# Loading 112 of 128 rows of four token blocks ahead, and 16 later, at the seam of a fused long convolution and soft mixture of experts

## The chip, the cores and the metric

The program runs on one core of a Trainium2 chip. The metric is the device time of one execution in microseconds, the median of three: 898.48 us (896.55 to 900.4) before the change.

## What is computed

A long convolution with a gate makes the tokens; a soft mixture of experts, whose softmaxes run over all tokens (dispatch) and over all slots (combine), works on them.

```python
# x, v: (4, 11456, 128); h_filt: (11456, 128) from pos_emb, w1, w2 and a decay
u = x * v
y = irfft(rfft(u, 2*S) * rfft(h_filt, 2*S))[:S]
x = (x * y).reshape(45824, 128)
logits = x @ phi                                  # (45824, 32): 8 experts with 4 slots
d = softmax(logits, axis=0)                       # over the tokens
slot_input = (d.T @ x).reshape(8, 4, 128)
slot_out = relu(slot_input @ w1[e]) @ w2[e]       # F = 1024
out = softmax(logits, axis=1) @ slot_out
```

## The kernel before

**Convolution.** The 128 features are worked in 8 groups of 16 (`CG`), by transforms in four steps that run as matrix products. Step g of the outer loop (`for g in range(G + 1)`, L476) does the first two steps of group g and the last two of group g - 1. The large region `T` holds a group's spectra; the third step `p3` (L353) reads it and writes `E`; the fourth, `p4` (L397), reads `E`, once for each of seven row blocks `rb` in the order `ORDER`; `p4_gate` or `p4_gate_apart` multiply its result with the input `x`; `p4_out` (L449) writes the products to `scr` in DRAM, a buffer in pieces, each of which holds all 128 features of a range of tokens. Group g fills rows 16 g to 16 g + 15 of each piece. In the last turn, g = 8, no first step is left: all third steps of the last group run (L537), and then the seven fourth steps.

**Mixture.** The 45,824 tokens are 23 blocks of 16 tiles of 128 tokens (the last has 6). A block is loaded from `scr` as 128 rows (features) of 2048 tokens, 8192 B a row. `Moe.load` (L685) does it for a block and a range of rows, with one DMA for each piece that the block touches, on SP's queue. Blocks 0 to 4 have buffers in the region of the table `W`, which is free earlier (`ahead_buf`, L659). Blocks 5 to 8 have theirs in the region of `T` (`xreg`, made by `places`, L675), which is free when the last third step has read `T`; block 9 has one in `E`. Blocks from 10 on use the buffers of blocks 5 to 9 again. The expert weights `w1` go into the region of blocks 0 to 4 when those have been used.

For blocks 0 to 4 rows 0 to 111 (groups 0 to 6, `D - CG` = 112) are loaded by `weights` (L661) before the last third steps, and rows 112 to 127 by `ahead` (L716) when the last group's products are in `scr`. `ahead(t)` runs behind the products of row block number t: blocks 0 and 1 at t = 1, blocks 2 to 5 at t = 2, 6 and 7 at t = 3, 8 at t = 4, 9 at t = 5. Blocks 5 to 9 are loaded there whole.

The generator `_moe` (L726) holds the dispatch: for pairs of blocks, `logits` (L768) multiplies the block with `phi`, a running maximum, exponentials, `turn` (L697), which transposes the block on TensorE, and `dispatch` (L858), which adds up the slots. The logits of the pair 0, 1 are computed between the sixth and the seventh fourth step, the others behind the seventh; VectorE's gates of the sixth and seventh fourth step come behind the first logits. `fetch` (L949) follows each `turn`: behind blocks 0 to 3 it loads `w1` (L664), behind block 4 `w2` (L667), and from block 5 on block i + 5.

**Order.** Computing instructions keep the order in which they are written (`keep_in_program_order`). The DMAs go through SP's queue in an order that the framework's planner makes from its own costs, and which follows the program for the most part. Dependences are kept by semaphores that the framework sets. The edge rows `ex` (L571) are 128 x 12 floats, 6 KB.

Of the kernel before, what the change touches and what calls it, by code (L numbers as in the profile page):

```python
# [17 lines left out]
B, S, D = 4, 11456, 128  # L18
# [11 lines left out]
CG = D // G  # L30
# [33 lines left out]
def conv_part(ctx, tc, cp, moe, xf, vf, xi, xe, pos, w1, w2, win, t1x, t1h, wt, t3, t4, hs, scr):  # L64
# [190 lines left out]
    def p1_x(g, u):  # L255
        if g == 0 and u < NU // 2:
            xt = moe.E[:, J * N1 + 8 * RP * u :][:, : 8 * RP].rearrange("p (c q r) -> p c q r", c=2, q=4)
        elif g == 0 and u >= NU - 6:
            xt = m_half(g, u).rearrange("p (c q r) -> p c q r", c=2, q=4)
        else:  # L260
            xt = ld.tile([128, 2, 4, RP], F32, tag="ld", name=f"x_{g}_{u}")
        inorder(nc.sync.dma_start(out=xt, in_=xf[g, u]))
        xts[u] = xt
# [66 lines left out]
    def p1(g, u, sd, large=False):  # L330
        first_out(g, u, first(g, u, sd, large))
# [52 lines left out]
    def p4_load(g, rb):  # L384
        t = spare[next(turns) % len(spare)]
        inorder(nc.sync.dma_start(out=t, in_=xi[g, rb]))
        return t
# [88 lines left out]
    for g in range(G + 1):  # L476

        if g == 0:
            for u in range(NU):
                p1(g, u, sds.pop(u))  # L480
                if u in (9, 11):
                    p1_x(1, PRE + 2 + (u - 9) // 2)
        elif g < G:
            if not pso:
                first_ps.close()
                pso.append(conv_ps.enter_context(tc.tile_pool(name="pso", bufs=2, space=bass.MemoryType.PSUM)))
            def third(us, larges):
                for u, large in zip(us, larges):
                    p3(g - 1, u, large)
                    if u + 2 < NU and u + 2 not in sds:  # L490
                        sds[u + 2] = p1_sd(g, u + 2, nc.vector)

            def behind(u):
                w = u + 6
                if w < NU:
                    p1_x(g, w)
                elif w < NU + PRE and g + 1 < G:
                    p1_x(g + 1, w - NU)

            def spectrum(i0, i1):  # L500
                for k in range(11 * i0, 11 * i1, 11):
                    inorder(nc.sync.dma_start(out=Hs[:HP, k : k + 11], in_=hs[g - 1, :, k : k + 11]))

            large = g > 1
            ps = [first(g, u, sds[u], not large) for u in range(2)]
            third(range(2), (large, large))
            for u in range(2):
                first_out(g, u, ps[u])
                behind(u)
            for w in range(PRE + HV, NU):  # L510
                p1_v(g, w)
            third(range(2, 4), (large, large))
            for u in range(2, 4):
                p1(g, u, sds[u], not large)
                behind(u)
            for b in range(1, NU // 4):
                if b > 1:
                    spectrum(4 * b - 8, 5 * b - 6)
                us = range(4 * b, 4 * b + 4)
                third(us, (large, large, not large, not large))  # L520
                for u in us:
                    p1(g, u, sds[u], large == (u % 4 < 2))
                    behind(u)
            if g + 1 < G:
                for w in range(PRE):
                    p1_v(g + 1, w)
        else:
            x0, x1, x2 = [sm.tile([128, PW], F32, tag="m", name=f"xl_{i}", bufs=3) for i in range(3)]
            spare = [x0, x1, x2] + [spare[i % 2] for i in (next(turns), next(turns))] + [x0, x2]
            turns = count()  # L530
            xvs = [p4_load(g - 1, rb) for rb in ORDER[:5]]
            moe.weights()
            conv_ps.close()
            moe.logit_banks()
            pso[0] = ctx.enter_context(tc.tile_pool(name="psl", bufs=3, space=bass.MemoryType.PSUM,
                                                    reuse_waits="tile"))
            for u in range(NU):  # L537
                p3(g - 1, u)
            moe.places()
            moe.steps = _moe(moe)  # L540
            next(moe.steps)

        sds = {}
        nxt_g = g + 1 if g + 1 < G else None

        def ahead(step):
            if nxt_g is None:
                return
            if step == 1:
                for u in range(PRE):  # L550
                    sds[u] = p1_sd(nxt_g, u, nc.vector)
            else:
                for u in range(PRE, PRE + 4):
                    p1_x(nxt_g, u)

        if 0 < g:
            ahead(1)
        ks = list(range(0, J, KB)) if g < G else []
        if g == 0:
            sds = next_sds  # L560
            for i, k in enumerate(ks):
                if k % HK == 0:
                    for w in range(k, min(J, k + HK), 4):
                        filter_last(w)
                p2(g, k)
                if i in (1, 5, 9, 13):
                    u = PRE + i // 4
                    sds[u] = p1_sd(1, u, nc.vector)
            continue
        ex = exs[g % 2]  # L570
        inorder(nc.sync.dma_start(out=ex, in_=xe[g - 1]))  # L571
        if g < G:
            xvs = {0: p4_load(g - 1, 0), APART: p4_halves(g - 1, APART), 2: p4_load(g - 1, 2)}
            vcs, done = {}, 0
            for what, n in STEPS:
                if what == "p2":
                    for _ in range(n):
                        p2(g, ks[done])
                        done += 1
                elif what != "gate":  # L580
                    pv = p4(g - 1, n, what)
                    if what:
                        vcs[n] = p4_copy(g - 1, n, pv)
                else:
                    if n == APART:
                        p4_gate_apart(n, xvs[n], pvs[n], vcs[n], ex)
                    else:
                        p4_gate(g - 1, n, xvs[n], pvs[n], vcs[n], ex)
                    if g < G - 1 and n == 5:
                        for u in range(PRE, PRE + HV):  # L590
                            p1_v(g + 1, u)
                    p4_out(g - 1, n, xvs[n])
                    if n == 0:
                        ahead(2)
                    if n in NEXT:
                        xvs[NEXT[n]] = p4_load(g - 1, NEXT[n])
                    if n == 2:
                        xvs[6] = p4_halves(g - 1, 6)
            assert done == len(ks)
            p4_rest(g - 1, ex)  # L600
            continue
        def last_gate(t, rb, xv, pv, vc):
            if t < 4:
                p4_gate(g - 1, rb, xv, pv, vc, ex)
            else:
                p4_gate_apart(rb, [xv[:, PW // 2 * w :][:, : PW // 2] for w in range(2)], pv, vc, ex)
            p4_out(g - 1, rb, xv)
            if t == 5:
                p4_rest(g - 1, ex)
            if t == 3:  # L610
                xvs.append(p4_load(g - 1, ORDER[6]))
            moe.ahead(t)
            if t == 1:
                xvs.append(p4_load(g - 1, ORDER[5]))

        for t, rb in enumerate(ORDER):
            p4(g - 1, rb, 0)
            if t == 6:
                next(moe.steps)
                last_gate(*held)  # L620
            pv = p4(g - 1, rb, 1)
            vc = p4_copy(g - 1, rb, pv)
            held = (t, rb, xvs.pop(0), pv, vc)
            if t == 4:
                moe.spot = wide[rb][:, 0, 2 * NJ : 2 * NJ + 8]
            if t >= 5:
                next(moe.steps)
            if t != 5:
                last_gate(*held)


class Moe:
# [83 lines left out]
    def ahead(self, t):  # L716

        if t == 0:
            make_identity(self.tc.nc, self.ident)
            self.tc.keep_in_program_order(self.tc.nc.vector.tensor_reduce(  # L720
                out=self.mask, in_=self.ident.rearrange("p (a s) -> p a s", a=4), axis=AX.X, op=ALU.add))
        for i in ((), (0, 1), (2, 3, 4, 5), (6, 7), (8,), (9,), ())[t]:
            self.load(i, D - CG if i < self.XB else 0)


def _moe(mo):  # L726
# [564 lines left out]
```

## Time and profile before

| what | us |
|---|---|
| median of three runs | 898.48 |
| the three runs | 896.55, 898.48, 900.4 |
| the profiled execution, time | 899.17 |
| the profiled execution, span from first to last instruction | 897.4 |
| TensorE (PE) busy in it | 858.3 (96%) |
| VectorE busy | 716.3 (80%) |
| ScalarE busy | 454.7 (51%) |
| GpSimd busy | 392.7 (44%) |

The profile is of one execution. Busy times say how much of the span an engine had an instruction at work; a busy share near 100% doesn't say that nothing waits, since it is a mean over stages. [...] The DMA share is the mean busy share of the 16 DMA engines, and can come out a little over 1 because transfers of one engine overlap. SP is the engine that issues the DMAs; its queue's rows are marked SPq.

### The profile page before, as it was taken

What the parts mean: (1) busy time and instruction counts of PE and PEld (TensorE: products, weight loads), DVE (VectorE), ACT (ScalarE), POOL (GpSimd) and SP (SyncE); (2) the same over time, 40 slices, a digit from 0 to 9 for tenths busy, and PEclk for the clock granted to TensorE, in tenths of its full rate; (3) what the DMA queues carried; (4) which work ended last, traced back from release to release, by engine and by line L of the source; (5) the groups of instructions that cost most, each with busy time, mean ns of one, the idle gap of its engine ahead of it and who ended that gap; (6) DMA issues with size and microseconds to landing.
All of it is one profiled execution on the core that took longest, in us unless ns stands there. A gap on an engine that the chain in (4) does not pass through costs nothing. (4 is left out here: it accounts for less than half of the span.)

```text
span 897.4 us, 37454 instructions
## 1 busy us (share of the span) xinstructions
PE 858.3 (96%) x16264; PEld 792.2 (88%) x16264; DVE 716.3 (80%) x1239; ACT 454.7 (51%) x971; POOL 392.7 (44%) x538
## 2 busy tenths in 40 slices
PE   9999999999999999999999999999999999599991
PEld 9998989999999999999999999999999987376640
DVE  5967966898899899979988998898697078396791
ACT  5775557316712841581175148216612548497761
POOL 4004850591096039207802940691096015395750
PEclk9999999999999999999999999999999999699996
DMA  9954675548647655874675567557527979893698
GB/s 328 396 185 132 209 231 168 159 132 261 200 128 225 214 159 167 257 210 125 191 249 163 148 212 248 162 147 247 169 60 214 256 224 382 335 317 122 265 417 367
DMA packets 96114, 197.02 MB, mean 220 GB/s; under 512 B 14649, under 2 KB 56539, under 8 KB 92750
## 3 DMA queue, kind: packets, MB, share of 16 engines
q1 hardware_dynamic: 95774, 194.50, 67.2%
q8 instruction: 128, 2.10, 1.0%
q14 instruction: 36, 0.29, 0.1%
q10 hardware_dynamic: 144, 0.07, 0.0%
q0 software_dynamic: 32, 0.07, 0.0%
HBM read 137.73 MB, written 56.86 MB: 217 GB/s over the span
## 5 line engine op out<-in xcount | busy, mean ns | idle before, releaser
L350 POOL TENSOR_TENSOR T<-m 111x256 f32<-111x256 f32 (+1 forms) x199 | 150.3, 755 | 344.1 <-DVE m L344 343.8
L344 DVE TENSOR_TENSOR m<-p,T 111x1024 f32<-111x1024 f32 (+1 forms) x175 | 200.4, 1205 | 14.8 <-POOL T L351 7.8
L360 PE MATMUL p<-tab,T 111*99 111x112 f32 x2048 | 205.4, 261 | 1.4 <-POOL T L351 0.3
L360 PEld LDWEIGHTS p<-tab,T 111*99 111x99 f32 x2048 | 198.8, 170 | 6.4 <-issue 1.6
L340 PE MATMUL p<-T,W 128*64 128x128 f32 (+1 forms) x3168 | 198.1, 276 | 0.3 <-issue 0.3
L420 ACT ACTIVATE vc<-p 128x416 f32<-128x416 f32 x112 | 51.8, 515 | 266.5 <-PE p L411 220.4
L340 PEld LDWEIGHTS p<-T,W 128*64 128x64 f32 (+1 forms) x3168 | 183.2, 127 | 2.2 <-issue 0.5
L411 PE MATMUL p<-tab,E 99*64 99x104 f32 x3584 | 176.0, 252 | 1.2 <-DVE E L373 0.6
L411 PEld LDWEIGHTS p<-tab,E 99*64 99x64 f32 x3584 | 168.2, 136 | 3.4 <-ACT vc L420 0.8
L375 ACT ACTIVATE E<-p 99x448 f32<-99x448 f32 x254 | 131.8, 575 | 64.3 <-PE p L360 58.2
L351 POOL TENSOR_TENSOR T<-m 111x256 f32<-111x256 f32 (+1 forms) x199 | 146.7, 737 | 0.0
L186 ACT ACTIVATE T<-p 128x396 f32<-128x396 f32 x240 | 100.2, 537 | 11.2 <-PE p L174 11.1
L174 PE MATMUL p<-tab1x,x 53*64 53x99 f32 x3648 | 86.8, 246 | 0.2 <-ACT E L224 0.2
L174 PEld LDWEIGHTS p<-tab1x,x 53*64 53x64 f32 x3648 | 79.8, 132 | 4.4 <-ACT E L224 0.4
L436 DVE TENSOR_TENSOR p<-p,vc 128x832 f32<-128x832 f32 x46 | 47.2, 1027 | 10.1 <-ACT vc L420 10.1
L268 DVE TENSOR_TENSOR x<-x,T 128x448 f32<-128x448 f32 x51 | 31.5, 618 | 20.3 <-DMA x<-in_xf_dram 12.6
L714 ACT ACTIVATE xreg<-pt 128x512 f32<-128x512 f32 (+1 forms) x68 | 35.0, 608 | 12.3 <-PE pt L708 12.2
L270 DVE TENSOR_TENSOR T<-x 128x224 f32<-128x224 f32 x102 | 39.2, 426 | 1.7
L274 DVE TENSOR_TENSOR x<-T 128x224 f32<-128x224 f32 x102 | 39.2, 425 | 1.8
L224 ACT ACTIVATE E<-fl 111x512 f32<-111x512 f32 (+1 forms) x50 | 26.8, 627 | 21.4 <-PE fl L218 21.4
L444 DVE TENSOR_TENSOR E<-p,E 128x824 f32<-128x824 f32 x36 | 36.6, 1017 | 1.2
L344 DVE TENSOR_TENSOR m<-p,E 111x1024 f32<-111x1024 f32 (+1 forms) x25 | 28.7, 1202 | 5.1 <-PE p L340 4.9
(156 smaller groups left out, 972.3 us busy)
## 6 DMA issues: line engine op xcount, KB each, us to landing
x<-in_xf_dram SPq DMA_DIRECT2D x114, 256.0 KB, 4.0
out_dram<-xreg SPq DMA_DIRECT2D x16, 1024.0 KB, 10.7
E<-in_xi_dram SPq DMA_DIRECT2D x37, 412.0 KB, 4.0
T<-in_vf_dram SPq DMA_DIRECT2D x65, 224.0 KB, 4.8
scr<-E SPq DMA_DIRECT2D x67, 206.0 KB, 3.8
T<-hs SPq DMA_DIRECT2D x63, 154.0 KB, 4.7
hs<-E SPq DMA_DIRECT2D x12, 784.0 KB, 4.6
mv<-in_vf_dram SPq DMA_DIRECT2D x42, 224.0 KB, 4.6
```

What stands on the lines that cost most here:

```text
L174: inorder(nc.tensor.matmul(ps[h][RP * d : RP * d + RP, i, s, :], lhsT=sd[js, i, s, d, :], rhs=tab1x[js, J * (s + d) : J * (s + d + 1)], st ...
L186: inorder(nc.scalar.activation(dst, src, AF.Copy))
L270: inorder(eng.tensor_tensor(out=vt[:, :, m : m + 2], in0=xr[:, :, 0:2], in1=xr[:, :, 2:4], op=op))
L340: inorder(nc.tensor.matmul(ps[ns, i].rearrange("p b c -> p (b c)"), lhsT=W[:, k0 + i, ns], rhs=Tf[:, :, k0 + i, :], start=True, stop=True, ...
L344: inorder(nc.vector.tensor_mul(m[:, :n].rearrange("p k s e c i -> p k s (e c i)").rearrange("p k s (b c) -> p k s b c", c=CG), ps[:, :n].u ...
L350: inorder(eng.tensor_tensor(out=Ty[:, 0], in0=m[:, :n, 0, 0], in1=m[:, :n, 1, 1], op=ALU.subtract))
L351: inorder(eng.tensor_tensor(out=Ty[:, 1], in0=m[:, :n, 1, 0], in1=m[:, :n, 0, 1], op=ALU.add))
L360: inorder(nc.tensor.matmul(pk[:, i, 2 * s : 2 * s + 2, :].rearrange("p q r -> p (q r)"), lhsT=T[0:N1, s, 2 * k + i, u // 2, :, u % 2], rhs ...
L375: inorder(nc.scalar.activation(dst, src, AF.Copy))
L411: inorder(nc.tensor.matmul(pv[RP * h : RP * h + RP, 2 * k + i, w, :], lhsT=E[:J, r, 2 - 2 * w + s, :], rhs=tab4[:, s, o : o + NJ], start=( ...
L420: inorder(nc.scalar.activation(vc[:, w], pv[:, :, 0, :], AF.Copy, scale=2.0 * w - 1.0))
L436: inorder(nc.vector.tensor_tensor(out=pw, in0=pw[:, 1:2].to_broadcast([128, 2, 4, NJ]), in1=vc, op=ALU.add))
```

## The change

The loads of rows 0 to 111 (seven groups) of blocks 5 to 8 are written right behind the last third step, where the region of `T` has become `xreg`. In `ahead`, where these blocks were loaded whole, only rows 112 to 127 are loaded, as for blocks 0 to 4. Block 9 is loaded whole as before. With the pieces that they touch, blocks 5 to 8 took 6 DMAs and now take 12.

```diff
@@ -537,6 +537,8 @@
             for u in range(NU):
                 p3(g - 1, u)
             moe.places()
+            for i in range(moe.XB, 2 * moe.XB - 1):
+                moe.load(i, 0, D - CG)
             moe.steps = _moe(moe)
             next(moe.steps)
 
@@ -720,7 +722,7 @@
             self.tc.keep_in_program_order(self.tc.nc.vector.tensor_reduce(
                 out=self.mask, in_=self.ident.rearrange("p (a s) -> p a s", a=4), axis=AX.X, op=ALU.add))
         for i in ((), (0, 1), (2, 3, 4, 5), (6, 7), (8,), (9,), ())[t]:
-            self.load(i, D - CG if i < self.XB else 0)
+            self.load(i, D - CG if i < 2 * self.XB - 1 else 0)
 
 
 def _moe(mo):
```

`XB` is 5, so the ranges are blocks 5 to 8, and i < 9.

## Rows read from the trace of the kernel before

**Rows 1.** The page, the span in 40 slices of 22.4 us, in tenths.

```profile
PE   9999999999999999999999999999999999599991
PEclk9999999999999999999999999999999999699996
DMA  9954675548647655874675567557527979893698
```

**Rows 2.** Chain of waits in time, 740 to 790: start us, us, what.

```profile
743.42 1.92 PE pl L774 x16
...
749.88 1.92 PE pl L774 x16
...
752.44 8.04 DMA ffw<-in_mw_dram
...
760.54 11.72 DMA xreg<-scr
...
772.40 1.97 PE pl L774 x8
...
782.38 1.92 PE pl L774 x16
```

**Rows 3.** Windows: length, busy by engine, then granted clock, DMA share, GB/s.

```profile
704.00:718.00 14.00, 13.44 (x188) 13.26 (x188) 0.94 (x3) 7.76 (x17) 0.29 (x3) 1.00 1.02 235
718.00:730.00 12.00, 12.00 (x272) 11.99 (x269) 8.91 (x11) 3.75 (x9) 0.00 (x0) 1.00 0.60 164
723.00:724.00 1.00, 1.00 (x28) 1.00 (x25) 0.24 (x2) 0.81 (x2) 0.00 (x0) 1.00 0.05 7
731.00:734.00 3.00, 3.00 (x43) 1.43 (x41) 1.41 (x3) 0.93 (x2) 1.75 (x3) 1.00 1.05 130
736.00:748.00 12.00, 11.80 (x238) 8.13 (x238) 10.70 (x18) 11.50 (x29) 5.95 (x6) 1.00 1.02 406
758.00:776.00 18.00, 8.46 (x164) 4.83 (x156) 8.34 (x15) 9.09 (x19) 9.75 (x13) 0.72 1.03 409
...
766.00:768.00 2.00, 0.00 (x0) 0.00 (x0) 0.00 (x0) 1.11 (x2) 0.74 (x1) 0.50 1.02 410
772.40:780.00 7.60, 6.82 (x79) 3.29 (x82) 3.07 (x6) 1.87 (x4) 0.00 (x0) 0.53 0.75 259
```

**Rows 4.** Timeline of SP's queue, 698 to 751: start us, us, line, DMA, count.

```profile
698.07 4.17 SPq L694 DMA_DIRECT2D ffw<-scr  x6
...
720.25 1.09 SPq L458 DMA_DIRECT2D scr<-xl  x2
723.28 0.33 SPq L694 DMA_DIRECT2D ffw<-scr  x1
...
727.67 3.02 SPq L694 DMA_DIRECT2D ffw<-scr  x5
...
747.56 2.36 SPq L458 DMA_DIRECT2D scr<-xl  x2
750.94 5.40 SPq L664 DMA_DIRECT2D ffw<-in_mw_dram  x8
```

**Rows 5.** Lines L571 (702 to 704) and L694 (724.5 to 726): issues, landing times.

```profile
L571 SPq DMA_DIRECT2D E<-in_xe_dram x1: 352/352/352, 703.0 to 703.0; - x1
...
DMA to landing us min/median/max: 15.5/15.5/15.5
...
L694 SPq DMA_DIRECT2D ffw<-scr x2: 501/542/582, 724.8 to 725.5; - x2
...
DMA to landing us min/median/max: 3.4/3.7/4.1
```

**Rows 6.** Timeline, PE: last third step, first logits, last work ahead of the wait.

```profile
712.83 0.55 PE L360 MATMUL p<-tab,T 111*99 111x112 f32 x4
...
731.35 1.92 PE L774 MATMUL pl<-ffw,aux 128*32 128x512 f32 x16
...
763.73 0.90 PE L708 MATMUL pt<-aux,xreg 64*128 64x64 f32 x22 [0.99 <-issue]
```

## The prediction, made before the changed kernel was run

> **What bounds the kernel now.** I began with the slices of the span [rows 1]: TensorE (PE) stands at 9 tenths nearly everywhere, with a hole to 5 in slice 35, where its granted clock is down to 6 tenths while the DMA engines stay at 9. The change works in this stretch and just ahead of it, so the rest of the 898 us is left alone. The chain of waits in order of time [rows 2] names the owner of the hole: from 752.44 to 772.26 us the chain is on DMA alone, 8.04 us on the first-layer expert weights and 11.72 us on a load of token rows, which is block 10; the logits of block 10 start at 772.40 when it lands. PE had finished at 764.63 (763.73 + 0.90 [rows 6]) and waited 7.8 us. [...] From one pair's logits to the next takes 10.0 us here (772.40 to 782.38), against 6.5 us in an undisturbed pair (743.42 to 749.88) [rows 2].
>
> The windows [rows 3] tell how the queue got there. It is full from 704 to 718 (share 1.02, but only 235 GB/s), has room from 718 to 730 (share 0.60, so 0.40 x 12 = 4.8 us of idle DMA time), and is full again to 776. Block 10 stands behind everything that SP issued before it, the expert weights included (first issue at 750.94 [rows 4]). So the question is not whether blocks 5 to 8 come earlier, since PE does not wait for them now; it is whether the change takes DMA time away ahead of block 10, and whether anything small gets stuck behind the early loads.
>
> **The change, in DMA time.** Blocks 5 to 8 are 4 x 128 rows of 8192 B, 4.19 MB. Now they go as 128-row loads in the full stretch; at the 406 GB/s of 736 to 748 [rows 3] they take 10.3 us, and this is removed. Added early: 112 rows of each, 3.67 MB. What pace have 112-row loads? The kernel has some: the early loads of blocks 0 to 4 have this very form; the last six, issued from 698.07 [rows 4], are most of the traffic of 704 to 718, at 235 GB/s with the engines full [rows 3]. I take that row: 15.6 us. The bound below is the 406 GB/s of 128-row loads, 9.0 us. Added late: 16 rows of each, 0.52 MB; in 731 to 734, when the 16-row loads of blocks 2 to 4 (issued from 727.67 [rows 4]) are the traffic, the pace is 130 GB/s at a share of 1.05 [rows 3], so 4.0 us (1.3 us at 406). Net: 15.6 + 4.0 - 10.3 = 9.3 us more DMA time. Splitting the rows makes the same bytes dearer.
>
> [...]
>
> Of the idle 4.8 us the early loads take all. They can be issued when the last third step has read T, at 712.83 + 0.55 = 713.4 [rows 6]; the queue is full to 718 anyway, so they run from 718 to 718 + 15.6 = 733.6. Six more issues of some 0.33 us each cost nothing, as SP issues nothing else between 713 and 720.25 [rows 4].
>
> **What stands behind the early loads.** All this goes through one SP queue, and it is served in order: a transfer of 6 KB (the edge rows, L571) issued at 703.0 behind the loads of blocks 1 to 4 (698.07 [rows 4]) took 15.5 us to land [rows 5]. So the first write of the last group's products, issued at 720.25, lands not at 723.28 (where the load that waits for it goes out [rows 4]) but behind the early loads, about 733.6 + 1.5 = 735.1 (0.5 to 3.0 us: its own 0.4 MB at 406 GB/s, up to the 3.0 us that it takes on an empty queue). From there the last rows of blocks 0 and 1 have to be loaded: now that takes from 723.28 to 725.5 + 4.1 = 729.6 [rows 4, 5], 6.3 us, so block 1 would be whole at 741.4. PE reaches the logits of blocks 0 and 1 at 731.35 and is at block 1 at 732.3 now [rows 6]; it would stand until 741.4, 9.1 us later, and everything on PE, VectorE and ScalarE behind it with it. So a new wait of 9 us appears 30 us ahead of the old one. It does not add to the old one, since the old one ends by the DMA queue; it eats it.
>
> Also queued behind: the other writes and last-row loads on SP. When SP waits for the first write's landing and the queue is empty, some DMA time is lost; today a hole of this kind is the slice 723 to 724 with a share of 0.05 [rows 3]. I take 1.0 us (0 if the planner issues the second write ahead, up to 2). The expert weights follow the last product write (747.56 [rows 4]). Its product waits for PE and would be done some 11 us later, about 754, while the queue has work to about 760, so this order costs nothing unless PE is 4 us later still.
>
> **The sum.** Block 10 is ready at 772.4 + 9.3 - 4.8 + 1.0 = 777.9. PE is there at 764.6 + 9.1 + 1.9 = 775.6 (1.9 us is the lower clock after the new wait: 10.0 us for the pair at the lower clock, less the 8.1 worked out next), so 2.3 us of the old wait are left; I take it that the clock stays up over so short a wait. The pair of blocks 10 and 11 takes 6.5 us, and 1.6 us more because block 11's 1.05 MB land 2.6 us behind block 10 while PE would be at it after 1.0: 8.1 us. The next pair begins at 777.9 + 8.1 = 786.0, against 782.38 now: 3.6 us later. From there the blocks come faster than PE uses them (2.10 MB at 409 GB/s, 5.1 us, for a pair of 6.5 us), and the remainder runs as now. The profiled execution has a span of 897.4 us and a time of 899.17, against the median of 898.48; the difference of 0.7 us is small beside the terms, and I add to the median: 898.5 + 3.6 = 902.1 us. That is 0.4% slower, and about 0.5% (4.5 us) is what a measurement of this kernel can tell from no change.
>
> **The rivals.** (a) Slower beyond doubt: the old wait stays long enough to bring the clock down. The forecast leaves 2.3 us of it, and the clock was at 0.50 in 766 to 768 with PE waiting from 764.63 [rows 3, 6], so this is near. Then the pair takes 10.0 us and not 8.1, and the next begins at 787.9: 5.5 us later, 904.0 us. It decides from the point where block 10 is more than some 2 us behind PE. It also covers the case that the write overtakes the early loads (PE not late, 13 us of wait at block 10: the same 787.9). With 2 us more of lost DMA time it is 906. For it: the closeness; against it: a PE later than I think closes the gap. Chance 0.33.
>
> (b) The early loads run as fast as whole ones. Then they take 9.0 us, the DMA sum is 9.0 + 4.0 - 10.3 - 4.8 + 1.0 = -1.1, block 10 is ready at 771.3, the logits of block 1 are 2.5 us late (727.0 + 1.5 + 6.3 = 734.8), PE waits 4.2 us at block 10, and the next pair begins at 781.3, or at 779.4 with the clock up: 1.1 to 3.0 us earlier, 895.5 to 897.4. If the late rows were also cheap, 2.7 us less: 893. For it: the 409 GB/s of whole loads from the same memory region; against it: 235 GB/s over 14 us in the very form. Chance 0.15. [...]
>
> (c) The change doesn't do what it says: the planner, which orders SP's queue by its own costs, puts the early loads behind the first writes. Then the DMA sum is the same 9.3 us, but the first logits are not late and little of the idle time is used; it ends as (a) or up to 4 us worse. If the loads went out only where the whole ones do now, the time would be 898 to 903. Chance 0.08.
>
> **How the numbers follow.** Forecast 0.39: 900.5 to 903. Slower (a) 0.33, (b) 0.15, (c) 0.08, and 0.05 for what I don't see. Predicted 902.1. For 8 in 10 the range takes in (b) at its lower end and (a) with lost DMA time and a 112-row pace a little under the row's: 894.5 to 907.5. Slower by over 0.5% (above 903.0): (a), half of (c) and a little of the forecast's edge, 0.37; faster (below 894.0): the far end of (b) and the unseen, 0.10; within 0.5%: 0.53.
>
> **What would show it.** In the profile of the changed kernel: six loads of token rows issued at 713 to 719; windows at about 235 GB/s to 733; the write at 720 landing after 733; PE waiting for the last rows of blocks 0 and 1 from 731 to about 741, with the clock down behind it; 16-row loads at 130 GB/s; the wait at block 10 shrunk to 0 to 3 us, ending at 777 to 779. I would be wrong if the early loads ran near 400 GB/s, if the write landed by 726, or if block 10 landed before 772.

## The result, and the profile after the change

The changed kernel takes 904.21 us (median of 20 runs, 899.91 to 910.55); the kernel before took 898.57 us beside it (20 runs, 895.16 to 902.06). The ratio is 1.0059, 95% interval 1.0044 to 1.0075: slower by 0.6%, about 5.3 us. The forecast was 902.1, and the result lies inside the range and just past the 0.5% bound on the slow side, to which the prediction had given a chance of 0.37, against 0.53 for within 0.5%. The profiled execution of the changed kernel took 899.91 us (span 898.1), the shortest of its 20. A second profiled execution, called the second profile below (run e1), took 902.62 (span 900.8) and is nearer to the median, so both are shown.

In the changed kernel the old line L774 is L776, L694 is L696, L708 is L710, L664 is L666. First the windows of the first profile (length, busy by engine, then granted clock, DMA share, GB/s), the answer to [rows 3]; the granted clock is that of TensorE, as a share of its full speed:

```profile
718.00:730.00 12.00, 9.15 (x199) 8.74 (x196) 8.12 (x9) 3.19 (x8) 0.00 (x0) 1.00 1.01 267
736.00:748.00 12.00, 11.88 (x220) 8.29 (x220) 10.44 (x19) 8.20 (x22) 3.83 (x7) 1.00 0.97 236
745.00:755.00 10.00, 9.75 (x211) 6.71 (x213) 8.34 (x15) 9.04 (x23) 4.72 (x4) 1.00 0.84 216
758.00:776.00 18.00, 11.61 (x244) 7.23 (x233) 10.94 (x18) 11.99 (x26) 11.55 (x13) 0.91 1.03 406
773.37:780.00 6.63, 5.92 (x60) 2.48 (x64) 3.07 (x6) 0.97 (x3) 2.46 (x5) 0.53 0.89 344
```

Three windows of the second profile:

```profile
718.00:730.00 12.00, 9.14 (x198) 8.73 (x194) 7.75 (x9) 3.27 (x8) 0.00 (x0) 1.00 1.03 254
731.00:734.00 3.00, 3.00 (x38) 3.00 (x36) 0.00 (x0) 0.00 (x0) 0.00 (x0) 0.50 0.91 298
750.00:755.00 5.00, 4.91 (x108) 3.13 (x108) 3.97 (x7) 4.96 (x13) 3.62 (x3) 1.00 0.76 153
```

The idle DMA time of 718 to 730 is gone: the share is 1.01 where it was 0.60 [rows 3]. The early loads fill it, at 267 GB/s (254 in the second profile). Two things are new. TensorE is busy for 9.15 of these 12 us, where it was busy for all 12. And from 745 to 755 the share is 0.84: after all that was added, the DMA engines now stand idle for part of the time right ahead of the expert weights.

SP's queue in the first profile (start us, us, line, DMA, count), the answer to [rows 4]:

```profile
713.81 2.66 SPq L696 DMA_DIRECT2D xreg<-scr  x6
...
720.61 4.90 SPq L458 DMA_DIRECT2D scr<-xl  x4
731.79 2.06 SPq L696 DMA_DIRECT2D ffw<-scr  x3
...
750.25 1.09 SPq L458 DMA_DIRECT2D scr<-xl  x2
751.43 6.98 SPq L666 DMA_DIRECT2D ffw<-in_mw_dram  x8
```

The early loads go out at 713.81. The four writes of the first two steps follow from 720.61, and the loads that need them go out at 731.79 and not at 723.28 [rows 4]. The chain of waits in order of time (start us, us, what), the answer to [rows 2], tells why, and what comes of it:

```profile
720.61 11.12 DMA scr<-xl
...
750.25 7.29 DMA scr<-xl
757.59 9.25 DMA ffw<-in_mw_dram
766.91 8.97 DMA xreg<-scr
```

The first write takes 11.12 us behind the early loads. Block 10 is still the last link, behind the weights, and these follow the write of the last rows (750.25). TensorE's timeline, first the first profile, then the second (start us, us, line, matmul, count, idle time before it and what ended it):

```profile
714.30 6.82 PE L411 MATMUL p<-tab,E 99*64 99x104 f32 x147 [0.56 <-DVE E L373]
722.07 5.93 PE L411 MATMUL p<-tab,E 99*64 99x104 f32 x127 [0.95 <-issue]
729.91 5.21 PE L411 MATMUL p<-tab,E 99*64 99x104 f32 x110 [1.90 <-issue]
735.06 2.01 PE L776 MATMUL pl<-ffw,aux 128*32 128x512 f32 x16
...
773.37 1.94 PE L776 MATMUL pl<-xreg,aux 128*32 128x512 f32 x8 [3.21 <-DMA xreg<-scr]
...
783.18 1.92 PE L776 MATMUL pl<-xreg,aux 128*32 128x512 f32 x16
```

```profile
722.44 5.93 PE L411 MATMUL p<-tab,E 99*64 99x104 f32 x127 [1.24 <-issue]
730.56 6.87 PE L411 MATMUL p<-tab,E 99*64 99x104 f32 x110 [2.18 <-issue]
738.36 1.92 PE L776 MATMUL pl<-ffw,aux 128*32 128x512 f32 x16 [0.93 <-issue]
...
776.58 1.94 PE L776 MATMUL pl<-xreg,aux 128*32 128x512 f32 x8 [3.26 <-DMA xreg<-scr]
...
786.12 1.92 PE L776 MATMUL pl<-xreg,aux 128*32 128x512 f32 x16
```

The first logits start 3.7 us late (735.06 for 731.35 [rows 6]) in the first profile and 7.0 us late in the second. In the fourth steps, L411, TensorE stands still after 147 and after 274 matmuls, for a reason that the profile calls issue, that is, it waits for nothing that the profile shows. These two standstills are 2.85 us in the first profile and 3.42 in the second, where the last 110 matmuls also take 6.87 us for 5.21, with the granted clock at 0.50 from 731 to 734 (1.00 in the first profile).

The 0.93 us ahead of the second profile's logits are called issue too, but they are a wait for a DMA. TensorE's weight-load queue stands at a semaphore of L776 for 2.08 us, from 736.22 to 738.30, and the last rows of block 0, whose load goes out at 734.99, land at 738.27. The line L776 from 730 to 740 shows it (ns, shortest/median/longest):

```profile
L776 PEldq EVENT_SEMAPHORE  x2: 51/1067/2083, 736.2 to 738.9; - x2
```

In the first profile the same load lands at 734.84, when TensorE is still in the fourth steps. So two things hold the first logits back, and they cover each other. Without the standstills TensorE would have been there some 17.4 us after the start of the fourth steps, as in the kernel before, at 731.7 and 731.8, and would have waited 3.1 and 6.5 us for these rows. This is an estimate that takes their landing as it was.

At block 10 TensorE waits 3.2 us where it waited 7.77, and the next pair starts 0.8 us (783.18) or 3.7 us (786.12) after the 782.38 of before [rows 2]. From there to the end of the span all is as before: 115.0 us before, 114.9 and 114.7 now.

### The profile page after: what moved, and what is told of

Same layout as the page of the kernel before. It is cut to its first block, busy times and chain, and to the rows that moved or that the text cites. A ratio compares the mean times of both kernels' runs of the same rounds, so it can differ in the third digit from the quotient of the medians.

```text
span 898.1 us, 37462 instructions
## 1 busy us (share of the span) xinstructions
PE 861.4 (96%) x16264; PEld 792.6 (88%) x16264; DVE 716.7 (80%) x1239; ACT 455.4 (51%) x971; POOL 393.1 (44%) x538
## 5 line engine op out<-in xcount | busy, mean ns | idle before, releaser
L411 PE MATMUL p<-tab,E 99*64 99x104 f32 x3584 | 175.5, 252 | 3.9 <-issue 2.9
L411 PEld LDWEIGHTS p<-tab,E 99*64 99x64 f32 x3584 | 167.2, 136 | 6.5 <-issue 4.3
L1125 PE MATMUL pw<-cs,so 32*128 32x512 f32 (+2 forms) x192 | 32.9, 633 | 0.7 <-DVE xreg L1132 0.7
```

Of the source, the lines that this page charges most:

```text
L411: inorder(nc.tensor.matmul(pv[RP * h : RP * h + RP, 2 * k + i, w, :], lhsT=E[:J, r, 2 - 2 * w + s, :], rhs=tab4[:, s, o : o + NJ], start=( ...
L1125: inorder(nc.tensor.matmul(po[:, :na].rearrange("p k t -> p (k t)"), lhsT=so[NSLOT * a : NSLOT * a + NSLOT], rhs=ct[NSLOT * a : NSLOT * a ...
```

## The experiments

Two theories stood against each other at first. D: splitting the loads makes the same bytes dearer in DMA time, and block 10 stands behind all of it. Q: what counts is the small write and the last rows of blocks 0 and 1, stuck behind the early loads. Every run was compared with the kernel before on the same chip.

The start of the last fourth steps moves from one execution to another (713.7 to 717.1 us, below), so the table gives TensorE's milestones from that start. The next pair is that of blocks 12 and 13. All columns in us but the ratio.

| kernel | time | ratio to before, 95% | start | first logits | block 10 | next pair |
|---|---|---|---|---|---|---|
| before | 898.5 to 899.3 | 1 | 713.94 | 17.41 | 58.46 | 68.44 |
| before, second profile (e8) | | | 714.42 | 17.30 | 57.88 | 67.80 |
| changed | 904.21 | 1.0059 (1.0044 to 1.0075) | 714.30 | 20.76 | 59.07 | 68.88 |
| changed, second profile (e1) | 904.33 | 1.0050 (1.0035 to 1.0064) | 714.38 | 23.98 | 62.20 | 71.74 |
| e2 split, not moved | 906.78 | 1.0081 (1.0064 to 1.0097) | 714.79 | 17.31 | 64.03 | 74.28 |
| e3 early rows for nothing | 894.96 | 0.9949 (0.9934 to 0.9965) | 717.08 | 17.30 | 53.25 | 61.14 |
| e4 early loads of 128 rows | 900.04 | 1.0011 (0.9997 to 1.0024) | 715.62 | 18.99 | 57.35 | 67.15 |
| e5 two blocks split | 901.59 | 1.0013 (0.9996 to 1.0031) | 715.30 | 18.97 | 58.21 | 68.99 |
| e6 weights late | 893.32 | 0.9930 (0.9909 to 0.9950) | 713.69 | 17.30 | 49.45 | 55.93 |
| e7 weights late, and the change | 898.69 | 0.9998 (0.9978 to 1.0019) | 714.88 | 23.11 | 55.79 | 61.97 |
| e9 delay alone | 902.82 | 1.0032 (1.0015 to 1.0049) | 716.69 | 23.07 | 60.35 | 70.22 |
| e10 weights late, and the delay | 899.82 | 1.0011 (0.9998 to 1.0024) | 716.33 | 23.08 | 56.03 | 62.20 |
| e11 weights later still | 893.78 | 0.9939 (0.9921 to 0.9957) | 713.72 | 17.30 | 50.51 | 56.68 |

**e1, the changed kernel again.**

> The changed kernel once more, for another execution's profile, since the first one shown (899.91 us) was the fastest of its twenty. Theory D (the split makes the loads dearer in DMA time, and block 10 stands behind them): 903 to 906 us, and in an execution near that time the windows 718 to 734 show 112-row loads at 230 to 250 GB/s and block 10's logits start at 776 to 779. Theory Q (what counts is the small write and the last rows of blocks 0 and 1 that stand behind the early loads): 903 to 906 too, but block 10's logits start within 1 us of 772.4 and the lost time is on PE from 720 to 745.

The ratio, 1.0050, agrees with the first within the intervals, and the run gave the second profile shown above. Block 10's logits start at 776.58, in D's range and not in Q's, and 718 to 734 moves 259 GB/s, a little above D's 250. But the 6.6 us that the first logits are late, counted from the start of the fourth steps, lie where Q looks.

**e2, the split without the move.** The 112 rows and the 16 rows are loaded one after the other where the whole block was loaded. So that the planner keeps this, the loads of blocks 5 and up are also held in program order (not shown).

```
...
-            self.load(i, D - CG if i < self.XB else 0)
+            if self.XB <= i < 2 * self.XB - 1:
+                self.load(i, 0, D - CG)
+            self.load(i, D - CG if i < 2 * self.XB - 1 else 0)
```

> Only the split: blocks 5 to 8 are loaded as 112 and 16 rows where they were loaded whole, nothing is moved ahead. Theory D: 15.6 + 4.0 - 10.3 = 9.3 us more DMA time in the full stretch, none of it into the idle of 718 to 730, so block 10 is ready at 781 to 782 and the time is 906 to 910 us. Theory Q: nothing stands ahead of the first write, so no change, 898 to 899 us.

It is the slowest of all, 7.3 us above before by the ratio. TensorE and one window:

```profile
736.00:748.00 12.00, 11.80 (x228) 8.14 (x226) 9.95 (x17) 11.03 (x27) 5.91 (x6) 1.00 1.03 270
```

```profile
778.82 1.93 PE L778 MATMUL pl<-xreg,aux 128*32 128x512 f32 x8 [11.09 <-DMA xreg<-scr]
```

With the engines full, 736 to 748 moves 270 GB/s where whole loads moved 406 [rows 3], and TensorE, which is not late here (first logits at 17.31), waits 11.09 us at block 10. So the split alone costs more than the whole change, as D has it, though block 10's logits come 2 to 3 us sooner than D's 781 to 782. Moving the larger part ahead into the idle time gives 2.4 us back (906.78 to 904.33).

**e3, the early rows for nothing.** GpSimd fills rows 0 to 111 of blocks 5 to 8 with zeros in place of the early loads; the late 16 rows stay.

```
-            for i in range(moe.XB, 2 * moe.XB - 1):
-                moe.load(i, 0, D - CG)
+            for t in moe.xbuf[: moe.XB - 1]:
+                inorder(nc.gpsimd.memset(t[: D - CG], 0.0))
```

> The early loads are left out: GpSimd, idle there, sets these rows to zero, and only the 16 last rows of blocks 5 to 8 are loaded (the dispatch of these blocks is so computed from wrong rows). Theory D: the DMA sum is 4.0 - 10.3 = -6.3 us, block 10 is ready at about 766, PE waits for it 1 to 2 us at full clock, and the next pair begins about 8 us earlier than before: 889 to 892 us. Theory Q: the first logits are on time, the rest as in the kernel before: 898 us.

4.6 us faster than before by the ratio, between the two theories. There is no DMA wait at block 10 any more (53.25), and the fourth steps run through without a standstill (17.30):

```profile
770.33 1.07 PE L776 MATMUL pl<-xreg,aux 128*32 128x512 f32 x8
```

A standstill of 1.85 us comes later here (762.57, in the logits of blocks 8 and 9), with the engines full (a share of 1.03 from 758 to 776), and is a part of what is missing to D's 889 to 892. This run is the most that the idea could have given here: the early loads cost 9 us against loads that cost nothing.

**e4, early loads of 128 rows.** The early loads read 128 rows of the same 8192 B from a table in DRAM and not 112 rows of the products; then the 16 late rows as in the change. The rows of blocks 5 to 8 are then mostly not the tokens. The part of `load` that takes `src` isn't shown.

```
...
-                moe.load(i, 0, D - CG)
+                moe.load(i, src=wt.rearrange("p k n -> p (k n)"))
```

> The early loads take 128 rows from a table of 128 rows in DRAM in place of 112 rows of tokens, the same DMA count and row lengths, the 16 last rows are loaded over them later (blocks 5 to 8 so hold wrong values in 112 rows). 14% more bytes, but the whole form. Theory D with the pace of 112-row loads as its cause: early 10.3 us in place of 15.6, so block 10 is ready at 772 to 773, the first logits are 3 to 4 us late in place of 9: 896 to 900 us. If the pace is not the cause (theory Q, or loads of any form are slow here): 903 to 906 us as with the change.

900.04 us, within the measurement of before. It moves more bytes early, in less time:

```profile
718.00:730.00 12.00, 11.65 (x254) 11.25 (x252) 7.66 (x9) 3.70 (x8) 0.00 (x0) 1.00 1.02 403
```

403 GB/s for 128 rows, against 267 and 254 for 112 rows in the same window of the two profiles. The price of the change hangs on the pace of the 112-row form: take it away, and 0.39% of 0.50 go (1.0011 against the 1.0050 of e1). The table is other memory than the products, so the run changes the source beside the number of rows; whole loads of the products run at 406 [rows 3], which speaks for the number. The size of the packets is not the cause: in the packet records of the traces one of 8192 B takes 0.50 and 0.52 us (medians) in this window of the two profiles, and 0.31 us here and in 736 to 748 of before.

**e5, two blocks.** Only blocks 5 and 6 are split and early.

```
-            for i in range(moe.XB, 2 * moe.XB - 1):
+            for i in range(moe.XB, moe.XB + 2):
                 moe.load(i, 0, D - CG)
...
-            self.load(i, D - CG if i < 2 * self.XB - 1 else 0)
+            self.load(i, D - CG if i < self.XB + 2 else 0)
```

> The kernel before with only blocks 5 and 6 split: their rows of seven groups are loaded behind the last third step, their last group's rows where the whole block was; blocks 7 and 8 stay whole and late, as before, and the weights keep their places. Theory D (split loads cost more DMA time, and block 10 stands behind all of it): half of the price, early 1.84 MB at 235 to 267 GB/s = 6.9 to 7.8 us, late 0.26 MB at 130 = 2.0, less 2.10 MB at 406 = 5.2, so +3.7 to +4.6 us of DMA time against 4.8 idle ones taken and about 1 lost where SP waits for the last rows of block 1: block 10 lands at most 1 us from before's, the first logits start 1 to 2 us later: 898 to 900.5, within 0.2% of before. Theory Q (what counts is that block 1's last rows stand behind early loads): the queue ahead of them is half as long, so half of the change's loss, 901 to 902. [...]

The time does not decide. The ratio (1.0013) is what D expected, but its interval reaches to 1.0031 and holds Q's half of the loss too, and the median lies in Q's range. The place of block 10 (58.21) speaks for D; the next pair is 0.6 us late, with a standstill of 2.62 us at 757.87 and a pair of 10.8 us behind the wait at block 10. The last rows of blocks 0 and 1 have landed by 732.1, before TensorE reaches the first logits. So the 1.6 us by which these are late are the standstill's after 147 matmuls, which is there with half of the early loads; the one after 274 is not:

```profile
723.50 10.84 PE L411 MATMUL p<-tab,E 99*64 99x104 f32 x237 [1.37 <-issue]
```

**e6 and e7, the wait at block 10 taken away.** The eleven weight transfers no longer stand ahead of block 10 but are spread behind the block loads from block 10 on; e6 is this in the kernel before, e7 in the changed kernel. In both, the weights and the loads of blocks 10 and up are also held in program order (not shown).

```
...
-        if i < XB - 1:
-            for e in range(2 * i, 2 * i + 2):
-                mo.load_w1(e)
-        elif i < XB:
-            for e in range(3):
-                mo.load_w2(e)
-        elif i + XB < NBL:
+        if i < XB:
+            return
+        if i + XB < NBL:
             mo.load(i + XB)
+            for w in range(11 * (i - XB) // (NBL - 2 * XB), 11 * (i - XB + 1) // (NBL - 2 * XB)):
+                mo.load_w1(w) if w < NEXP else mo.load_w2(w - NEXP)
```

> The kernel before with the eleven transfers of the experts' weights moved: none of them behind the pairs of blocks 0 to 9, where they stand ahead of blocks 10 to 14, but one of them behind each block's load from block 10 on. No early loads. Theory D (the wait at block 10 is the DMA queue's, and the queue ahead of it sets it): block 10 then lands 8 to 11 us sooner than at 772.4, TensorE waits there no longer, and the last logits come sooner by the wait removed and what a clock kept high gives, 7.8 to 11 us in all: 888 to 891. If the queue of weights and blocks (18.6 MB at 409 GB/s = 45.5 us from about 755) paces the later pairs instead, the gain is near 5: 892 to 894. If the wait at block 10 is not what the time hangs on: 897 to 899.

> The changed kernel with the same move of the weights behind the block loads from block 10 on. Theory D: with no DMA wait at block 10, nothing swallows the delay of the first logits (3.4 and 6.6 us in the two looks at the changed kernel), so it passes through to the end: 4 to 9 us slower than the kernel with the weights moved alone, 893 to 899. Rival (the early loads harm only by what they put ahead of block 10): equal to the kernel with the weights moved alone within 1.5 us, 888 to 892.

e6 and e11 are the fastest kernels of the study; e6 takes 893.32 us, 0.7% under before. Block 10 starts 9.0 us sooner after the start of the fourth steps (49.45 for 58.46), without a DMA wait. By the last logits 7.1 us of it are left (94.7 for 101.8 from the same start). 893 is above D's 888 to 891; it lies in the 892 to 894 that were expected if the queue of weights and blocks paces the later pairs. The share of 1.03 from 780 to 800 agrees with that, and TensorE stands still three times between 790 and 807 (0.78, 1.41, 1.78 us), with the share at 1.03. Window and timeline of e6:

```profile
780.00:800.00 20.00, 17.65 (x439) 12.95 (x439) 16.78 (x33) 16.41 (x38) 15.77 (x19) 1.00 1.03 402
```

```profile
763.14 1.92 PE L775 MATMUL pl<-xreg,aux 128*32 128x512 f32 x16
...
799.38 0.91 PE L709 MATMUL pt<-aux,xreg 64*128 64x64 f32 x23 [1.41 <-issue]
```

e7 is 0.68% slower than e6 (0.9998 against 0.9930), 6.1 us, in D's range. Its first logits are 5.8 us late (23.11 for 17.30), its block 10 6.3 us, its next pair 6.0. With the wait at block 10 gone, nothing is left that could swallow the delay of TensorE. Here the last rows of block 0 land at 735.2, 2.8 us before the first logits, so the standstills (3.55 us) and the lower clock behind them (0.60 from 731 to 734) reach further than the wait for the rows. Block 10 in e7:

```profile
770.67 1.92 PE L777 MATMUL pl<-xreg,aux 128*32 128x512 f32 x16
```

**e8, the kernel before once more.**

> The kernel before once more, one profile: whether the start of the last fourth steps (713.9 to 717.1 us in the looks so far) moves from execution to execution. Both theories expect the stretch from there to the first logits at 17.3 to 17.5 us, to block 10's logits at 58 to 59, to the next pair at 68 to 69. If the fourth steps start later than 716 here, the late start of the run without early transfers is the execution's own.

```profile
731.72 1.92 PE L774 MATMUL pl<-ffw,aux 128*32 128x512 f32 x16
...
772.30 1.94 PE L774 MATMUL pl<-xreg,aux 128*32 128x512 f32 x8 [7.35 <-DMA xreg<-scr]
```

The fourth steps start at 714.42 here. The milestones from that start agree with the first profile within 0.7 us. But the two profiles of the changed kernel differ by 3 us, so where the fourth steps are held up a single profile can be off by that much. The start itself differs by up to 3.4 us between kernels that have the same work ahead of it (716.3 to 717.1 in e3, e9 and e10); what moves it stays open.

**e9 and e10, the delay alone.** After e1 to e8 the standstill of TensorE stood as a cause beside the DMA time (theory S: the last rows are written later, and the weights and block 10 stand behind that write). Here the fourth steps are made longer by 5.8 us, with no early load at all: e9 in the kernel before, e10 in e6.

```
+                            for x in range(0 if g == G - 1 and s == 0 and rb in ORDER[1:5] else 1, 2):
+                                inorder(nc.tensor.matmul(
...
-                                rhs=tab4[:, s, o : o + NJ], start=(s == 0), stop=(s == 1),
+                                    rhs=tab4[:, s, o : o + NJ], start=(s == 0), stop=(s == 1 or x == 0),
```

> The kernel before with no early load, and with four of the last fourth steps made longer: every first matmul of a pair is done twice (64 more in the code, 128 in the trace, 5.8 us at 45 ns each), and the second does the sum, so the result stays. It gives TensorE the delay that it had in the changed kernel (3.4 us in one look, 6.6 in the other, where it stood still ahead of the first logits without any wait the profile shows), without any of the added DMA time. Theory S (that standstill sets the loss: the last rows are written later, the weights and block 10 stand behind that write): the first logits 5.8 us later, the weights' first load 3 to 5 us later, block 10 as much, and the time +3 to +5 us: 902 to 904. Theory D (DMA time sets it, and the 7.8 us wait at block 10 swallows a delay of TensorE): block 10 at most 1 us later, the wait there near 2 to 3 us: 898.5 to 900.

> The same longer fourth steps in the kernel whose weights are loaded behind the blocks from block 10 on (893.3 us without the delay, 898.7 with the early loads). There no DMA wait is left at block 10, so either theory lets the delay through: +5 to +6 us, 898.3 to 899.3. If it comes out there, the early loads' whole price in that kernel (+5.4) is what a delay of TensorE of their size costs. If it stays within 2 us of 893.3, something else than TensorE's delay makes the early loads dear in that kernel, and the DMA queue is what is left.

SP and TensorE in e9:

```profile
755.82 5.62 SPq L665 DMA_DIRECT2D ffw<-in_mw_dram  x8
```

```profile
739.76 1.92 PE L775 MATMUL pl<-ffw,aux 128*32 128x512 f32 x16
...
777.04 1.94 PE L775 MATMUL pl<-xreg,aux 128*32 128x512 f32 x8 [1.65 <-ACT xreg L715]
...
786.91 1.92 PE L775 MATMUL pl<-xreg,aux 128*32 128x512 f32 x16
```

Neither theory was right by itself. The 5.8 us cost 2.9 us (1.0032), at the foot of S's range and above D's. From the start of the fourth steps the first logits are 5.7 us late, the weights' first load 2.1 us (39.13 for 37.00), block 10 1.9 us: by block 10 the old wait has swallowed some two thirds of it. What goes through has two reasons that end together. The weights stand behind the write of rows that TensorE delays, and block 10's last load lands at 776.90. But TensorE also loses 1.01 and 1.53 us in two more standstills on the way (767.52 and 774.48), and ScalarE's copies behind its late transposes end at 776.94, which is what the profile names. In e10 the whole delay goes through, and a little more: 0.81% (1.0011 against 0.9930), 7.3 us, with block 10 6.6 us later. That is about as much as the early loads cost in e7 (6.1), at about the same delay of the first logits (23.08 and 23.11). So in that kernel the early loads' price can be the delay of TensorE alone, whatever makes it. Block 10 in e10:

```profile
772.36 1.92 PE L776 MATMUL pl<-xreg,aux 128*32 128x512 f32 x16
```

**e11, the weights later still.** The first eight from block 12 on, the next three behind the last block. The edit against e6:

```
+    def due(i):
+        return max(0, NEXP * (i - XB - 2) // (NBL - 2 * XB - 2))
...
-            for w in range(11 * (i - XB) // (NBL - 2 * XB), 11 * (i - XB + 1) // (NBL - 2 * XB)):
+            for w in range(due(i), due(i + 1)):
...
```

> The kernel with the weights behind the block loads once more, with the eight first weights spread from block 12 to the last block, and the next three behind the last block. The kernel with them from block 10 on lost 4.0 us to standstills of TensorE that the profile names issue, while the DMA share was 1.03 from 780 to 800 us. If these come from the full DMA queue, as theory S has it, a thinner queue leaves 1 to 3 us less of them: 890 to 892.5. If the queue stays full whatever the order (the block loads come as fast as buffers come free), the same within 1 us: 892.5 to 894. If a weight is now late for the experts: 895 or more.

893.78 us, the same as e6. The DMA share from 780 to 800 is 1.03 here too, as was expected if block loads go out as fast as buffers come free, and the standstills stay:

```profile
799.89 0.90 PE L709 MATMUL pt<-aux,xreg 64*128 64x64 f32 x23 [1.34 <-issue]
```

## Why the prediction was right in its sign and near in its size

**What bounds the kernel: right.** After the change the chain still ends on the weights and block 10, and no other stage moved: from the next pair to the end the spans agree within 0.3 us.

**The early loads cost more than whole ones: right, and shown.** The forecast took 235 GB/s from [rows 3]; the window 718 to 730 shows 267 and 254. The first early load goes out at 713.8, and the last lands at 731.3 in the first profile (issued at 716.1, 15.2 us to land) and at 734.4 in the second (717.8, 16.6 us), where the forecast had 733.6. Splitting in place (e2) costs 7.3 us; the forecast had 9.3 us of added DMA time. Rival (b), early loads at the pace of whole ones, is out. e4 comes near to what it would have meant, and can't be told from before (1.0011, to 1.0024); the forecast for (b) was 1 to 3 us faster, with 9.0 us for 112 rows, where e4 loads 128, 10.3 us at the same pace. Rival (c) is out too: SP issues the early loads ahead of the first writes.

**The first write stands behind the early loads: right.** 735.1 was forecast. The chain has it landing at 731.7 in the first profile (720.61 + 11.12) and at 734.9 in the second.

**A new wait of 9 us for the last rows of blocks 0 and 1: right in kind, too long, and hidden by what the forecast doesn't have.** This is the step that failed first. "Block 1 would be whole at 741.4" came from the 6.3 us that the loads take after the first write in the kernel before. But the planner put the second step's writes out with the first's (four writes in one row at 720.61, where there were two), so the loads of both blocks went out together at 731.79, and block 1 was whole 4 us after the write, at 735.9 in the first profile and 738.9 in the second. The forecast also has no standstills. With them TensorE comes to the first logits late by itself, and waits for block 0's rows 0 and 0.93 us; without them it would have waited some 3.1 and 6.5 us, by the estimate above. The first logits are 3.7 and 7.0 us late for the 9.1 forecast, and no run here tells for the changed kernel how much of that one of the two reasons would have made alone. e5 has a standstill without the wait (1.6 us late), e4 a standstill of 0.26 us and 0.67 us of the wait (1.6 us late).

**"This order costs nothing unless PE is 4 us later still": wrong.** The forecast let the queue have work until 760, so that the write of the last rows, late by TensorE, would not matter to the weights behind it. The share of 0.84 from 745 to 755 in the first profile, and of 0.76 from 750 to 755 in the second (0.97 there in before), shows the queue running dry in part: the weights wait for that write, go out at 751.43 and 754.60, and block 10 follows them by 22 us in both. e9, with TensorE late and no early load, has the weights 2.1 us late and is 2.9 us slower, though there TensorE's own lateness ends at the same moment. The idle time taken in 718 to 730 is in part given back here.

**The wait left at block 10 and the clock: the wait right, the clock wrong.** 2.3 us were forecast, 3.2 measured in both profiles. The forecast took it that the clock would stay up over so short a wait; the rows show 0.53 from 773.37 to 780, as in [rows 3] after 7.8 us, and the pair takes 9.8 us (first profile) and 9.5 (second) and not 8.1. This is what rival (a) had: 10.0 for the pair, and with it 904.0 us.

**The sum.** The forecast's next pair was 3.6 us late; the two profiles show 0.8 and 3.7, the median of all runs 5.3. That the second profile comes so near is luck: block 10 starts 1.3 us earlier than forecast (776.58 for 777.9), and its pair takes 1.4 us longer (9.5 for 8.1). The profiled executions are among the shorter executions of their kernel (899.91 of a median of 904.21, 902.62 of 904.33), so what the longer ones add, some 1.7 us over the second profile, no profile here shows. A delay of TensorE that differs from execution to execution, as it does between the two profiles, would do it, and so would a later start of the fourth steps, as in e3, e9 and e10; that is argued, not shown. How the 5.3 us divide between the DMA time and TensorE's delay is not shown either: e2 has 7.3 us from the split alone, e9 2.9 from a delay alone, and in the changed kernel both act through the same queue.

## What to carry to other kernels

Before a load is moved into idle DMA time, price its new form: 112 rows of 8 KB went at two thirds of the pace of 128 (254 and 267 GB/s against 403), and the split alone cost more (e2, 7.3 us) than the idle time was worth (4.8 us). Then ask which small writes and loads stand in the queue behind it, and what else uses the DMA engines in that stretch. Where the profile calls a wait issue, look at the semaphores of the engine's queue and at the landings before taking it for a wait without a reason. When the bound is a queue, look first at what stands in it without being due: the weights, first used 52 us after block 10's logits in before (824.42), stood ahead of it, and putting them behind gave 0.7%, at least as much as the early loads would have given had they been free (e3, 0.5%, intervals overlapping).

## What the runs showed of the hardware that was not expected

**The transfers over 112 partitions were slow for their bytes.** 254 and 267 GB/s with the engines full (shares of 1.03 and 1.01), against 403 to 406 for 128 partitions with the same 8192 B to a row (1.02). Why is open; packets of the same 8192 B took longer, 0.50 and 0.52 us against 0.31.

**In the fourth steps TensorE stood still at fixed places of its program, with the DMA share at 0.81 to 1.03.** After 147 and 274 matmuls in both profiles and in e7 (shares of 1.01, 1.03 and 1.02 from 718 to 730), after 147 in e5 (0.81); in before, e2, e3 and e6, with room in the DMA queue (a share of 0.51 to 0.63 from 718 to 730), the same instructions run through. From the one place to the next are 127 matmuls, as many weight loads and two waits on semaphores, 256 instructions in all. The page's list of queues has a queue of kind instruction with 128 packets and 2.10 MB, 16 KB each. In the trace such packets lie just ahead of the end of these standstills. In the first profile one packet lies in 727.3 to 728.7, none in 728.7 to 729.9, and TensorE goes on at 729.91, 1.30 us after the packet's end at 728.61; the standstill before it ends at 722.07, 1.38 us after a packet's end at 720.69. Packets by queue, first window, then second:

```profile
q1 hardware_dynamic: 72, 0.36, 95.6%
q8 instruction: 1, 0.02, 5.6%
```

```profile
q1 hardware_dynamic: 192, 0.33, 93.5%
```

In e6 a packet lies in 796.8 to 798, none from there to 799.38, where TensorE goes on. The kernel before has it too: a packet in 761 to 762.4, none in 763 to 763.8, and TensorE goes on at 763.73 after 0.99 us of issue [rows 6], with the share at 1.03 [rows 3]. Whether TensorE waited for these packets was not shown: no run here says what they hold or takes them out of the way. Full engines are not enough for a standstill: from 736 to 748 in before the share is 1.02, and TensorE is busy for 11.80 of 12 us [rows 3]; e4, with 128-row loads and a share of 1.02, has one standstill of 0.26 us in the fourth steps. And two short ones of before (0.38 us at 808.70, 0.25 at 818.69) fall where the share is 0.51 (806 to 809) and 0.50 (817 to 819).
